# Attention with gates and a multiplicative feed-forward block: quarter products, seven for eight, and blocks of 512 tokens

## The chip, the core and the metric

The kernel runs on one core of a Trainium2 chip. A core has TensorE (matmul, in the profile PE, its weight loads PEld), VectorE (DVE), ScalarE (ACT), GpSimd (POOL) and SyncE (SP, which here issues the DMA transfers). TensorE writes to PSUM, eight banks of 512 f32 columns on 128 partitions; VectorE and ScalarE read PSUM and SBUF. The metric is the device time of one execution in microseconds; lower is better.

## The reference

All in f32, except that the four weight matrices arrive as 8-byte numbers:

```python
f = 1 / (1 + exp(-f_logit))                       # (4, 8, 768, 48)
for t in range(S):
    state = f[t] * state + outer(k[t], v[t])      # one 48 x 48 state for each of 4 x 8 heads
    y[t] = q[t] @ state
x = y, heads side by side                         # 3072 tokens x 384
out = ((x @ w1) * (x @ w2)) @ w3 @ w_out          # 384 -> 1024 -> 1024 -> 384
```

## The kernel before

The sequence is cut into 24 chunks of 128 tokens (`NU`). For a chunk, `attention(u)` makes running products of the gates by two scans on VectorE (L263, L285), scales q and k with them (L279, L293), multiplies K by Q on TensorE (`pa`, L302), copies (L311) and masks the result on GpSimd (L317), multiplies by v and by the state (`py`, L346, L352), and moves the state on (`pk`, L328; `pd`, L368; `S`, L383 and L384). The result goes to `xt` by DMA (or, for the first block, by TensorE through a permutation, L423).

The weights come as 8-byte words and are turned into f32 by ScalarE and VectorE (`fetch`, L566 to L583). w3 and w_out are multiplied once into `wc` (`fold`, L636), so that the feed-forward block has two steps:

- up (L455): for each of 8 groups of 128 hidden features (`jc`) and each of w1 and w2 (`which`), three products, over 384 rows, into one PSUM bank `f`. ScalarE copies the first result (`a`, L464) and VectorE multiplies the second by it (`ab`, L471).
- down (L503): for each 128 tokens, eight products of 384 columns into a bank; ScalarE copies the sum (L516) and SyncE stores it.

Tokens go through it in eight blocks of 384. In the first two blocks the lower half of the hidden features is done chunk by chunk, in products of 128 columns, since a chunk is ready before its block is; all else takes 384 columns. In f32 each product of the code is two instructions on TensorE. PSUM holds `pa` (two banks), `pk`, `pd`, `py` and three banks `f`.

What sets the order is `Plan`: every piece of work is a task with an engine, a cost, tasks that it depends on, a priority and slots that it takes and frees. At each step the task that could start first by the given costs is taken, at equal times the one of lower priority number; the instructions are then written out in that order, so that each engine's queue is fixed at build time and runs in order, with semaphores between the engines.

## Time and profile before

| | us |
|---|---|
| median of 3 runs | 549.43 |
| lowest, highest | 548.67, 550.79 |
| the profiled execution | 546.54 |
| its span, first to last instruction | 544.7 |
| TensorE busy | 522.3 (96%) |
| VectorE busy | 223.1 (41%) |
| ScalarE busy | 164.3 (30%) |

Rows of a group read: line, engine, operation, output from inputs, shapes, count, then busy time in us, mean ns of one, and the engine's idle time before them with what ended it. Rows of the chain or of a timeline begin with start and length in us. Rows of a table of stretches give the stretch, its length, and for PE, PEld, DVE, ACT and POOL the busy us with the number of instructions; then the granted TensorE clock as a share, the DMA share and GB/s.

### The profile page before, as it was taken

To read this page: it belongs to the slowest core of one execution; us is meant where nothing else is said; L and a number is where in the kernel's file an instruction comes from. 1 tells how busy PE (TensorE), PEld (TensorE's weight loads), DVE (VectorE), ACT (ScalarE), POOL (GpSimd) and SP (SyncE) were. 2 spreads that over 40 slices of the span, in tenths; PEclk is the share of its full clock that TensorE was granted. 3 is DMA by queue.
4 is the path that set the end of the run, shared out by engine and by line. 5 is a ranking of instruction groups with operands and counts; after the bars stand their busy time and mean duration, and the time that the engine had idled before them with its cause. 6 is when DMAs were issued, how large, how long until landed. Compare 5 with 4: busy or idle time off the path is not lost.

```text
span 544.7 us, 7379 instructions
## 1 busy us (share of the span) xinstructions
PE 522.3 (96%) x2838; PEld 345.3 (63%) x2838; DVE 223.1 (41%) x351; ACT 164.3 (30%) x325; POOL 40.0 (7%) x45
## 2 busy tenths in 40 slices
PE   2769999999999999999999999999999999999995
PEld 2759866666677965765567556755665555555553
DVE  7699999999767410561326111311011101100100
ACT  3658576542445311441125112311211111111110
POOL 5102010011102000120001000300000000000000
PEclk9999999999999999999999999999999999999998
DMA  6999667754435101330131002100200020000001
GB/s 179 226 238 258 212 228 248 228 159 134 134 113 149 48 0 48 105 110 0 26 91 59 1 10 67 41 1 0 74 16 1 14 58 16 0 14 30 0 16 34
DMA packets 30284, 46.13 MB, mean 85 GB/s; under 512 B 5536, under 2 KB 19744, under 8 KB 29216
## 3 DMA queue, kind: packets, MB, share of 16 engines
q1 hardware_dynamic: 30240, 45.57, 28.8%
q8 instruction: 24, 0.39, 0.3%
q14 instruction: 20, 0.16, 0.1%
HBM read 36.70 MB, written 4.72 MB: 76 GB/s over the span
## 4 chain that ended last, share of the span: by engine, by line
PE 92%; DMA 4%; POOL 1%; SPq 1%; DVE 0%; issue 0%; ACT 0%; POOLq 0%; ACTq 0%
PE f L455 46%; PE f L503 23%; PE f L636 8%; PE pa L302 4%; PE py L346 4%; PE py L352 4%; DMA raw<-in_w_dram 3%; PE pd L368 2%; PE pk L328 2%; DMA q<-in_q_dram 1%; SPq L250 0%; SPq L241 0%; POOL k L196 0%; POOL q L195 0%; PE f L423 0%
## 5 line engine op out<-in xcount | busy, mean ns | idle before, releaser
L455 PE MATMUL f<-xt,w 128*128 128x384 f32 (+1 forms) x960 | 256.3, 427 | 3.0 <-DVE w L583 2.8
L455 PEld LDWEIGHTS f<-xt,w 128*128 128x128 f32 x960 | 161.2, 193 | 89.7 <-DVE w L583 3.0
L503 PE MATMUL f<-wc,ab 128*128 128x384 f32 x384 | 126.2, 486 | 0.0
L471 DVE TENSOR_TENSOR ab<-f,a 128x384 f32<-128x384 f32 (+1 forms) x80 | 37.8, 474 | 204.1 <-PE f L455 203.8
L503 PEld LDWEIGHTS f<-wc,ab 128*128 128x128 f32 x384 | 72.4, 190 | 49.0
L464 ACT COPY a<-f 128x384 f32<-128x384 f32 (+1 forms) x80 | 33.1, 414 | 183.1 <-PE f L455 181.6
L317 POOL TENSOR_SCALAR_AFFINE_SELECT A<-A 128x1024 f32<-128x1024 f32 x24 | 33.1, 1378 | 312.0 <-ACT A L311 312.0
L636 PE MATMUL f<-wos,w3s 128*128 128x384 f32 x128 | 42.9, 488 | 0.0
L516 ACT COPY o<-f 128x384 f32<-128x384 f32 x24 | 11.5, 478 | 85.8 <-PE f L503 85.8
L279 DVE TENSOR_TENSOR Q<-q,fwd 112x512 f32<-112x512 f32 x24 | 18.9, 789 | 41.8 <-PE py L352 41.8
L263 DVE TENSOR_TENSOR_SCAN fwd<-gate,floor 112x512 f32<-112x512 f32 x24 | 31.1, 1294 | 10.1 <-ACT gate L255 8.4
L636 PEld LDWEIGHTS f<-wos,w3s 128*128 128x128 f32 x128 | 23.7, 190 | 14.9
L302 PE MATMUL pa<-Q,K 48*128 48x128 f32 x384 | 29.7, 297 | 1.8 <-DVE K L293 1.8
L285 DVE TENSOR_TENSOR_SCAN bwd<-gate,back 112x512 f32<-112x512 f32 x24 | 31.0, 1293 | 0.8
L302 PEld LDWEIGHTS pa<-Q,K 48*128 48x128 f32 x384 | 25.0, 199 | 7.6 <-issue 4.8
L311 ACT COPY A<-pa 128x1024 f32<-128x1024 f32 x24 | 24.2, 1009 | 16.8 <-PE pa L302 16.6
L346 PE MATMUL py<-A,vt 128*48 128x128 f32 (+1 forms) x384 | 27.2, 284 | 1.3 <-POOL A L317 1.3
L346 PEld LDWEIGHTS py<-A,vt 128*48 128x48 f32 (+1 forms) x384 | 21.3, 133 | 10.9 <-issue 8.7
L396 ACT ACTIVATE ys<-py 112x512 f32<-112x512 f32 x24 | 14.3, 595 | 34.8 <-PE py L352 20.5
L566 ACT ACTIVATE magnitude<-raw 128x1024 f32<-128x1024 f32 (+1 forms) x18 | 19.9, 1108 | 15.6 <-DMA raw<-in_w_dram 9.2
L352 PE MATMUL py<-Q,sb 112*112 112x128 f32 x160 | 22.6, 284 | 0.0
L578 DVE SCALAR_TENSOR_TENSOR rest<-raw 128x1024 uint32<-128x1024 uint32 (+1 forms) x18 | 20.9, 1159 | 0.3 <-DMA q<-in_q_dram 0.2
(55 smaller groups left out, 250.8 us busy)
## 6 DMA issues: line engine op xcount, KB each, us to landing
raw<-in_w_dram SPq DMA_DIRECT2D x8, 1024.0 KB, 5.8
f<-in_f_logit_dram SPq DMA_DIRECT2D x48, 96.0 KB, 2.5
q<-in_q_dram SPq DMA_DIRECT2D x48, 96.0 KB, 2.6
k<-in_k_dram SPq DMA_DIRECT2D x48, 96.0 KB, 2.4
vt<-in_v_dram SPq DMA_DIRECT2D x24, 192.0 KB, 2.6
out_dram<-o SPq DMA_DIRECT2D x24, 192.0 KB, 1.9
raw<-in_w_dram SPq DMA_DIRECT2D x4, 768.0 KB, 9.1
raw<-in_w_out_dram SPq DMA_DIRECT2D x4, 768.0 KB, 5.0
```

What stands on the lines that cost most here:

```text
L263: nc.vector.tensor_tensor_scan(s["P"], gate[u % 2][:, 0:NQ], floor, 0.0, ALU.mult, ALU.max)
L285: nc.vector.tensor_tensor_scan(s["R"][:, ::-1], gate[u % 2][:, NQ:0:-1], back[:, ::-1], 0.0, ALU.mult, ALU.max)
L302: nc.tensor.matmul(s["pa"][:, par, cols], lhsT=s["K"][rows(par), cols], rhs=s["Q"][rows(par), cols], start=True, stop=True,)
L311: nc.scalar.copy(s["A"].rearrange("p r h c -> p r (h c)"), s["pa"])
L317: nc.gpsimd.affine_select(out=a, in_=a, pattern=[[0, H], [1, C]], compare_op=ALU.is_ge, fill=0.0, base=0, channel_multiplier=-1,)
L346: nc.tensor.matmul(s["py"][64 * par : 64 * par + w, hp], lhsT=s["v"][:, h * D : h * D + w], rhs=s["A"][:, par, hp], start=(hp == 0), stop= ...
L352: nc.tensor.matmul(s["py"][:, hp], lhsT=sb[(u - 1) % 2][:, hp], rhs=s["Q"][:, hp * C : hp * C + C], start=False, stop=True, skip_group_che ...
L455: nc.tensor.matmul(s["pu", jc, which, c0][:, 0:nt], lhsT=up_weights(w12, which, kc, jc), rhs=s["xt"][:, kc, cols], start=(kc == 0), stop=( ...
L464: nc.scalar.copy(s["a", jc, c0][:, 0:nt], s["pu", jc, 0, c0][:, 0:nt])
L471: nc.vector.tensor_tensor(s["ab"][jc][:, cols], s["pu", jc, 1, c0][:, 0:nt], s["a", jc, c0][:, 0:nt], ALU.mult)
L503: nc.tensor.matmul(s["po", i], lhsT=s["ab"][jc][:, i * P : i * P + P], rhs=wc[:, jc], start=(jc == 0), stop=(jc == KF - 1),)
L636: nc.tensor.matmul(w3s["p", jc], lhsT=w3s[jc][:, 0, kc * P : kc * P + P], rhs=wos[:, kc], start=(kc == 0), stop=(kc == KF - 1),)
```

## The change

Blocks are 512 tokens, six of them. From block 1 on, the up products of two groups of hidden features (`jc` and `jc + 4`) and of w1 or w2 are made as one unit, `seven(jc, which)`. The 512 tokens are cut into two halves of 256, the two feature groups are the other two halves, and the first two of the three 128-row slices of the input are the halves of the contraction. The four quarter results then come from seven quarter products instead of eight (Winograd's form of Strassen's scheme): m1 to m7, four sums of token quarters (`xs`, L552 of the new code), made once per block, and sums of weight quarters (`w12t`, L953), made once. The third slice of the input takes no part in the scheme and is added by plain products inside m2, m7, m4 and m3, so a unit has 11 products of 256 columns. Three PSUM banks X, Y, Z are used; between products VectorE adds m1 to the banks: u2 after m6 (L605), u3 after m7 (L608), then the results c22, c21, c12 (L619), and c11 by ScalarE or, for w2, as a multiplication (L614). For w2 the results are multiplied by those of w1 (L623). Block 0 uses plain products, and half of block 1 too.

The down step takes 256 tokens at a time, as two halves of 128, the 1024 hidden features as two halves of four groups, and the 384 output columns as two halves of 192: seven times four products of 192 columns, with four sums of hidden quarters for each (`abs_`, L716), sums of `wc` made once (`wct`, L967), and five additions of 192 columns on VectorE (L731 to L765).

`place`, one SBUF tile of 13312 columns, holds the buffers of the weight loading first and those sums later, so the weight sums wait for the last conversion. There are four banks `f` instead of three; `pd` shares the bank of `pk`; k has two buffers instead of three.

Three places of the new order. All rows are those of TensorE (L455, L503 before; L481 after, for all products) or VectorE; an entry in brackets is a wait on another engine's semaphore.

TensorE before, from the last up group to the down step of the last block:

```order
L455 MATMUL f<-xt,w_59 128x384 [waits DVE_49]
L455 MATMUL f<-xt,w_59 128x384 x2
L455 MATMUL f<-xt,w_59 128x384 [waits Activation_49]
L455 MATMUL f<-xt,w_59 128x384 x2
L503 MATMUL f<-wc,ab 128x384 [waits DVE_49]
L503 MATMUL f<-wc,ab 128x384 x6
L503 MATMUL f<-wc,ab 128x384 [waits DVE_49]
```

A wait stands before every third product, for a bank; the last group's eighth down product waits for its own hidden features.

TensorE now, one unit in the middle of block 4 (`w_59` are the weights, `place` the sums). The rows are m2 (two), m7 (two), m1 and m6 of the next unit, m4 (two), m3 (two), and m5 of the next unit:

```order
L481 MATMUL f<-xt,w_59 128x256 [waits Activation_49]
L481 MATMUL f<-xt,w_59 128x256
L481 MATMUL f<-place 128x256
L481 MATMUL f<-xt,w_59 128x256
L481 MATMUL f<-xt,w_59 128x256 [waits DVE_49]
L481 MATMUL f<-place 128x256 [waits DVE_49]
L481 MATMUL f<-xt,place 128x256 [waits DVE_49]
L481 MATMUL f<-xt,place 128x256
L481 MATMUL f<-place,w_59 128x256 [waits DVE_49]
L481 MATMUL f<-xt,w_59 128x256
L481 MATMUL f<-place 128x256 [waits DVE_49]
```

Between m7 and m4, which waits for u3, stand the two first products of the next unit. VectorE at that place, from u3 of a unit of w2 (L608) to u3 of the next:

```order
L608 TENSOR_TENSOR place<-f,a 128x256 [waits PE_49]
L619 TENSOR_TENSOR place<-f,place 128x256 [waits DVE_49]
L623 TENSOR_TENSOR ab<-ab,place 128x256 [waits DVE_49]
L605 TENSOR_TENSOR place<-f,a 128x256 [waits PE_49,Activation_49]
L619 TENSOR_TENSOR a<-f,a 128x256 [waits PE_49]
L623 TENSOR_TENSOR ab<-ab,a 128x256 [waits DVE_49]
L619 TENSOR_TENSOR place<-f,place 128x256 [waits PE_49]
L623 TENSOR_TENSOR ab<-ab,place 128x256 [waits DVE_49]
L608 TENSOR_TENSOR place<-f,a 128x256 [waits PE_49]
```

No work of the attention stands between them here. At the end of block 4, TensorE goes from the last unit (m4, m3) to the down step; its first row is m1 of the down step, which was put ahead of m4:

```order
L481 MATMUL f<-wc,ab 128x192 x3
L481 MATMUL f<-xt,place 128x256 [waits DVE_49]
L481 MATMUL f<-xt,place 128x256
L481 MATMUL f<-place,w_59 128x256 [waits DVE_49]
L481 MATMUL f<-xt,w_59 128x256
L481 MATMUL f<-wc,ab 128x192 [waits Activation_49]
L481 MATMUL f<-wc,ab 128x192 x2
L481 MATMUL f<-wc,ab 128x192 [waits DVE_49]
L481 MATMUL f<-place 128x192 [waits DVE_49]
L481 MATMUL f<-place 128x192 x7
```

VectorE there, c12 of the last unit, its multiplication, and the operand sums of the down step:

```order
L619 TENSOR_TENSOR place<-f,place 128x256 [waits PE_49]
L623 TENSOR_TENSOR ab<-ab,place 128x256 [waits DVE_49]
L716 TENSOR_TENSOR place<-ab 128x512
L716 TENSOR_TENSOR place<-place,ab 128x512 [waits DVE_49]
L716 TENSOR_TENSOR place<-ab,place 128x512 [waits DVE_49]
```

The fourth product of m2 waits for the multiplication, and m6 for the second of the sums; before, the down products waited for one multiplication and no sum.

The diff, cut to its core (`X`, `Y`, `Z` are banks, `wt` a weight quarter, `tw` a sum of weight quarters, `quarter` a token quarter; the down step's m1 to m7 have four products each and the same form):

```diff
-TB = 384
+TB = 512
-NAB = 20
+NF = 4
+DH = DM // 2
+TH = TB // 2
+KH = KF // 2
...
+def place_of(jc):
+    return jc % KH * 2 + jc // KH
...
-    raws = ctx.enter_context(tc.tile_pool(name="raws", bufs=NRAW))
-    abp = ctx.enter_context(tc.tile_pool(name="abp", bufs=NAB))
+    abp = ctx.enter_context(tc.tile_pool(name="abp", bufs=4))
+    outs = ctx.enter_context(tc.tile_pool(name="outs", bufs=4))
-    ps_f = ctx.enter_context(tc.tile_pool(name="ps_f", bufs=3, space=PSUM))
+    ps_f = ctx.enter_context(tc.tile_pool(name="ps_f", bufs=NF, space=PSUM))
...
+    place = keep.tile([P, 13312], F32, name="place")
...
+    raws = [at(2048 * i, 2048).bitcast(U32) for i in range(NRAW)]
+    magnitudes = [at(6144 + 1024 * i, 1024) for i in range(2)]
+    w3_rows = [at(8192 + 1024 * i, 1, 1024) for i in range(2)]
+    wos = at(10240, KF, DM)
+    w12t = place[:, 0:5120].rearrange("p (w t c) -> p w t c", w=2, t=5)
+    xs = at(5120, 4, TH)
+    wct = [at(6144 + KH * DH * i, KH, DH) for i in range(4)]
+    ups = {(nm, i): at(a + 2 * TH * i, TH) for nm, a in (("u2", 9216), ("u3", 9216 + TH)) for i in range(2)}
+    abs_ = [at(10240 + KH * P * i, KH, P) for i in range(4)]
...
-                s["pd"] = ps.tile([R, HP, D], F32, name="pd")
+                s["pd"] = ps.tile([P, HP, R], F32, name="pk")[0:R, :, 0:D]
...
+        def sums():
+            for i in range(4):
+                def emit(i=i):
+                    a11, a12, a21, a22 = quarter(0, 0), quarter(1, 0), quarter(0, 1), quarter(1, 1)
+                    x, y, op = (
+                        (a21, a22, ALU.add), (xs[:, 0], a11, ALU.subtract), (a11, a21, ALU.subtract),
+                        (a12, xs[:, 1], ALU.subtract),
+                    )[i]
+                    nc.vector.tensor_tensor(xs[:, i], x, y, op)
+                deps = [tk[n * UB + c]["x"] for c in range(UB)] if i == 0 else [s["S", i - 1]]
+                last = [q[nm] for q in upq[-KF:] for nm in ("m5", "m6", "m7", "m3")] if i == 0 else []
+                s["S", i] = plan.add("DVE", 0.43, emit, deps + last + w12_sums[-1:], 100 * n + 30)
...
+            def m1():
+                three(bank("X"), [wt(0, 0)], [quarter(0, 0)])
+            def k1():
+                q["a"] = work.tile([P, TB], F32, name="a")[:, 0:TH]
+                nc.scalar.copy(q["a"], q["X"])
+            def m6():
+                three(bank("Y"), [tw(1)], [xs[:, 1]])
+            def m5():
+                three(bank("Z"), [tw(0)], [xs[:, 0]])
+            def m2():
+                three(q["X"], [wt(1, 0), wt(2, 0)], [quarter(1, 0), quarter(2, 0)], False)
+            def m7():
+                three(q["Y"], [tw(2), wt(2, 1)], [xs[:, 2], quarter(2, 1)], False)
+            def m4():
+                three(q["Y"], [tw(3), tw(4)], [quarter(1, 1), quarter(2, 1)], False)
+            def m3():
+                three(q["Z"], [wt(1, 1), wt(2, 1)], [xs[:, 3], quarter(2, 0)], False)
+            def u2():
+                nc.vector.tensor_tensor(ups["u2", k], q["Y"], q["a"], ALU.add)
+            def u3():
+                nc.vector.tensor_tensor(ups["u3", k], q["Y"], q["a"], ALU.add)
+            def c11():
+                if which == 0:
+                    nc.scalar.copy(to(0, 0), q["X"])
+                else:
+                    nc.vector.tensor_tensor(to(0, 0), q["X"], to(0, 0), ALU.mult)
+            def ended(tok, half, bank_, more):
+                def emit():
+                    m = more()
+                    nc.vector.tensor_tensor(m if which else to(tok, half), q[bank_], m, ALU.add)
+                return emit
+            def times(tok, half, more):
+                return lambda: nc.vector.tensor_tensor(to(tok, half), to(tok, half), more(), ALU.mult)
...
+            ready = [tk[n * UB + c]["x"] for c in range(UB)] + pieces[0] + pieces[1]
+            pe("m1", one_, m1, ready + [s["S", 3]] + old(1, "m7"), 0, takes=["f"])
+            q["k1"] = plan.add("ACT", 0.38, k1, [q["m1"]], -200, takes=["a"])
+            pe("m6", one_, m6, [q["m1"]], -1, takes=["f"])
+            pe("m5", one_, m5, [q["m6"]], -1, takes=["f"])
+            dve("u2", u2, [q["k1"], q["m6"]] + old(2, "e12"))
+            pe("m2", two_, m2, [q["k1"], q["m5"]], -5)
+            if which == 0:
+                q["c11"] = takes_ab(jc, plan.add("ACT", 0.38, c11, [q["m2"]], -200, frees=[q["m1"]]))
+            else:
+                dve("c11", c11, [q["m2"]] + old(1, "c11"), frees=[q["m1"]])
+            pe("m7", two_, m7, [q["u2"], q["m2"]], -5)
+            dve("u3", u3, [q["m7"]] + old(2, "e22"))
+            dve("c22", ended(1, 1, "Z", third), [q["u3"], q["m5"], q["c11"]])
+            pe("m4", two_, m4, [q["u3"]], -6)
+            dve("c21", ended(1, 0, "Y", first), [q["m4"], q["c11"]], frees=[q["m6"]])
+            pe("m3", two_, m3, [q["c22"], q["m4"]], -6)
+            dve("c12", ended(0, 1, "Z", second), [q["m3"]], frees=[q["m5"]])
+            if which == 1:
+                for nm, tok, half, more in (("22", 1, 1, third), ("21", 1, 0, first), ("12", 0, 1, second)):
+                    dve("e" + nm, times(tok, half, more), [q["c" + nm]] + old(1, "c" + nm))
+                s["done"][place_of(jc) // KH].extend([q["c11"], q["e22"], q["e21"], q["e12"]])
+            else:
+                for nm in ("22", "21", "12"):
+                    q["e" + nm] = q["c" + nm]
+            q["e21"]["frees"].append(q["k1"])
+            s["up"] += [q[nm] for nm in ("m1", "m2", "m7", "m4", "m3")]
+        if n == 0:
             for c in range(UB):
-                part(c, c + 1, range(KF // 2))
-            part(0, UB, range(KF // 2, KF))
+                part(c, c + 1, range(KH))
+            part(0, UB, range(KH, KF))
         else:
-            part(0, UB, range(KF))
+            if n == 1:
+                for c in range(0, UB, 2):
+                    part(c, c + 2, [jc + half * KH for half in range(2) for jc in range(KH // 2)])
+            for jc in range(KH // 2 if n == 1 else 0, KH):
+                seven(jc, 0)
+                seven(jc, 1)
 
...
+            def sum_(j):
+                def emit():
+                    a11, a21 = quarter_(0, 0), quarter_(1, 0)
+                    if j == 0:
+                        x, y, op = a21, quarter_(1, 1), ALU.add
+                    elif j == 1:
+                        x, y, op = abs_[0], a11, ALU.subtract
+                    elif j == 2:
+                        x, y, op = a11, a21, ALU.subtract
+                    else:
+                        x, y, op = quarter_(0, 1), abs_[1], ALU.subtract
+                    nc.vector.tensor_tensor(abs_[j], x, y, op)
+                return emit
...
+            got0, got1 = (s["done"][i] + wc_sums for i in range(2))
+            got = got0 + got1
+            dve("S0", 0.69, sum_(0), got + old("m5"), -30)
+            dve("S1", 0.69, sum_(1), [q["S0"]] + old("m6", "S3"), -30)
+            dve("S2", 0.69, sum_(2), got0 + old("m7"), -30)
+            dve("S3", 0.69, sum_(3), [q["S1"]] + old("m3"), -30)
+            pe("m1", m1, got0 + old("m7"), takes=["f"])
+            q["k1"] = plan.add("ACT", 0.33, k1, [q["m1"]] + old("c21"), -200)
+            pe("m6", m6, [q["m1"], q["S1"]], -1, takes=["f"])
+            dve("u2", 0.36, u2, [q["k1"], q["m6"]] + old("c12"))
+            pe("m2", m2, [q["k1"]] + got1, -2)
+            q["c11"] = plan.add("ACT", 0.33, c11, [q["m2"]] + stores[-4:-3], -200, frees=[q["m1"]])
+            pe("m7", m7, [q["u2"], q["S2"]], -3)
+            dve("u3", 0.36, u3, [q["m7"]] + old("c22"))
+            pe("m5", m5, [q["S0"], q["m2"], q["m6"]], -3, takes=["f"])
+            dve("c22", 0.36, c22, [q["m5"], q["u3"]] + stores[-4:-2])
+            pe("m4", m4, [q["u3"]], -4)
+            dve("c21", 0.36, c21, [q["m4"], q["c22"]], frees=[q["m6"]])
+            pe("m3", m3, [q["c22"], q["S3"], q["m4"]] + ([judged] if final else []), -4)
+            dve("c12", 0.36, c12, [q["m3"], q["c11"]], frees=[q["m5"]])
+            for half, deps in ((1, ("c21", "c22")), (0, ("c11", "c12"))):
+                stores.append(plan.add("SP", 0.45, store(half), [q[nm] for nm in deps], -10))
...
+        def sum_up(i, which):
+            def emit():
+                t = w12t[:, which]
+                b11, b21, b31, b12, b22, b32 = (
+                    w12[:, half, 2 * which + kc if kc < 2 else 4 + which] for half in range(2) for kc in range(KM)
+                )
+                x, y = ((b12, b11), (b22, t[:, 0]), (b22, b12), (b21, t[:, 1]), (b31, b32))[i]
+                nc.vector.tensor_tensor(t[:, i], x, y, ALU.subtract)
+            return emit
...
+                x, y = ((b12, b11), (b22, wct[0]), (b22, b12), (b21, wct[1]))[i]
```

More of the change, by code (lines that the diff above doesn't have):

```diff
@@ L448, in part @@
             nt = (c1 - c0) * C
-            cost = 6 * max(0.135, nt * 0.322 / TB)
+            cost = 6 * max(0.135, nt * 0.322 / 384)
             def up(jc, which):
@@ L564, in magnitude @@
         def magnitude():
-            s["m"] = flat(work.tile([P, 2 * NW], F32, name="magnitude"))
+            s["m"] = flat(magnitudes[order % 2])
             nc.scalar.activation(s["m"], s["hi"].bitcast(F32), AF.Abs)
```

248 lines of the change are left out of this document (174 added, 74 removed).

## The prediction

> **What bounds the kernel now.** I read the profile's page first (busy shares, chain of waits), then the table of stretches, then the groups of instructions by shape.
>
> ```profile
> span 544.7 us, 7379 instructions
> PE 522.3 (96%) x2838; PEld 345.3 (63%) x2838; DVE 223.1 (41%) x351; ACT 164.3 (30%) x325; POOL 40.0 (7%) x45
> PE 92%; DMA 4%; POOL 1%; SPq 1%; DVE 0%; issue 0%; ACT 0%; POOLq 0%; ACTq 0%
> ```
>
> Nine tenths of the chain that ended last is TensorE. A busy share can hide pipelining, so the stretches (busy us of each engine, granted clock, DMA share) matter more:
>
> ```profile
> 0.00:20.00 20.00, 8.38 (x70) 7.15 (x71) 13.47 (x23) 8.41 (x15) 8.03 (x22) 1.00 0.79 197
> 20.00:40.00 20.00, 14.72 (x144) 13.16 (x143) 16.81 (x26) 12.33 (x22) 1.49 (x1) 1.00 0.92 230
> 40.00:141.00 101.00, 100.98 (x688) 72.15 (x687) 96.61 (x137) 57.83 (x101) 11.56 (x8) 0.98 0.66 205
> 141.00:210.00 69.00, 69.00 (x537) 51.43 (x536) 32.54 (x60) 24.06 (x55) 6.05 (x5) 1.00 0.29 83
> 210.00:479.00 269.00, 269.00 (x1221) 166.29 (x1220) 59.21 (x100) 54.95 (x121) 12.88 (x9) 1.00 0.13 37
> 479.00:539.20 60.20, 60.18 (x187) 35.16 (x185) 4.46 (x8) 6.21 (x13) 0.00 (x0) 1.00 0.05 18
> 539.20:544.70 5.50, 0.00 (x0) 0.00 (x0) 0.00 (x0) 0.48 (x1) 0.00 (x0) 0.74 0.12 42
> ```
>
> From 40 us to 539.2 us TensorE (first busy figure) never stops; all its idle time, some 22 us, lies in the first 40 us and the last 5.5. So every microsecond of products removed after 40 us is a microsecond of the span, and so is every new wait of TensorE. VectorE (third figure) is nearly full from 40 to 141 us too, yet TensorE did not wait there. Afterwards it has room.
>
> **The price of a product by its columns.** Each product in the code is two instructions in the trace (480 up products, x960). The chain shows runs of them back to back; a group taken from 53 to 61.5 us gives the narrow ones:
>
> ```profile
> 448.23 30.96 PE f L455 x96
> 479.19 15.48 PE f L503 x48
> 48.50 1.34 PE f L423 x12
> L455 PE MATMUL f<-xt,w 128*128 128x128 f32 x75 | 8.5, 275 | 0.0
> L455 PEld LDWEIGHTS f<-xt,w 128*128 128x128 f32 x76 | 8.6, 192 | 0.1
> ```
>
> 384 columns: 30.96 / 96 = 322.5 ns per instruction. 128 columns: 8.5 / 75 = 113 ns. (The means, 275 here, contain the latency and overlap; busy time over count is the spacing.) Widths 192 and 256 do not occur. Bounds: in proportion to the columns, 161.3 and 215.0; on the straight line through the two rows, 165.4 and 217.8. I take the middle, 163.5 and 216.5; 512 columns in proportion, 430.
>
> The weight load, 192 ns in its row, might be thought to bind at 163.5. It does not: loads of that length followed each other every 113 ns in that very row, so they overlap. The Trainium skill, page "TensorE: Matmul & The Clock Gate", section "Back-to-back issue gap", speaks against this change: in a stream of loads and matmuls the spacing is set by both, 81 ns at 128 columns and 131 at 512. By that flat curve an instruction of 192 columns would cost an estimated 78% of one of 384, not half, and the change would lose. The row disagrees, 113 against 322.5 being 35%, so the sum goes by the row.
>
> **Products removed and added** (counts from the order of instructions, two instructions each):
> - before: 336 up products of 384 columns, 216.7 us; 144 of 128, 32.5; 192 down products of 384, 123.8. Together 373.0.
> - after: 96 of 128, 21.7; 24 of 512, 20.6; 444 of 256, 192.3; 336 down products of 192, 109.9. Together 344.5, so 28.5 less.
>
> The gain is below an eighth for three reasons: block 0 and half of block 1 still use plain products; the third slice of the 384 input rows takes no part, so a unit is 11 products instead of 12; only the down part gets 28 for 32. One chunk more goes through the moving products of L423, 1.34 us: net **27.2 us** less (24.9 to 30.1 by the bounds).
>
> **What is added on VectorE.** Rows by shape:
>
> ```profile
> L471 DVE TENSOR_TENSOR ab<-f,a 128x384 f32<-128x384 f32 x56 | 31.1, 556 | 193.1 <-PE f L455 192.7 <-ACT a L464 0.4
> L471 DVE TENSOR_TENSOR ab<-f,a 128x128 f32<-128x128 f32 x24 | 6.7, 283 | 11.1 <-PE f L455 11.1
> L383 DVE TENSOR_TENSOR S<-pd,S 112x192 f32<-112x192 f32 x16 | 5.6, 353 | 9.3 <-PE pd L368 9.3
> L263 DVE TENSOR_TENSOR_SCAN fwd<-gate,floor 112x512 f32<-112x512 f32 x24 | 31.1, 1294 | 10.1 <-ACT gate L255 8.4 <-ACT lasts L268 1.0
> L285 DVE TENSOR_TENSOR_SCAN bwd<-gate,back 112x512 f32<-112x512 f32 x24 | 31.0, 1293 | 0.8
> L293 DVE TENSOR_TENSOR K<-k,bwd 112x512 f32<-112x512 f32 x24 | 18.0, 750 | 4.9 <-DMA k<-in_k_dram 2.5 <-PE pa L302 1.8
> L279 DVE TENSOR_TENSOR Q<-q,fwd 112x512 f32<-112x512 f32 x24 | 18.9, 789 | 41.8 <-PE py L352 41.8
> ```
>
> 256 columns lie halfway between 283 and 556: 0.42 us. 192 columns: 0.353. 512: 0.75. The 36 units need 252 operations of 256 (five in a unit of w1, nine in one of w2): 106 us. Twelve down groups of four sums and five additions: 12 x (3.0 + 1.77) = 57. The remaining plain products 10.8, sums of tokens 20 x 0.42 = 8.4, sums of weights 10 x 0.75 and 4 x 1.1 = 12. Together 194, less the 37.8 of the two first rows: VectorE grows from 223 to about 379 us, some 71% of the new span. It stays below TensorE on average; what counts is where it comes last.
>
> **Inside a unit.** In the steady part one unit is 22 instructions, 22 x 216.5 = 4.76 us, with 5.9 us of VectorE per two units (9.5 us). The tightest wait is m4 for u3, a sum from PSUM that can start only when m7 is done. How long a hand-over takes:
>
> ```profile
> 447.75 0.49 PE L503 MATMUL f<-wc,ab 128*128 128x384 f32 x1
> 448.07 8.23 PE L455 MATMUL f<-xt,w 128*128 128x384 f32 x25
> 448.27 0.48 ACT L516 COPY o<-f 128x384 f32<-128x384 f32 x1 [4.68 <-PE f L503]
> ...
> 38.39 0.52 ACT kt L336
> 38.95 0.67 PE pd L368 x14
> ```
>
> The reader starts 0.20 us after the next product could start (448.27 against 448.07), and TensorE starts 0.04 after an engine that it waits for (38.91 to 38.95). So m4 is free 0.20 + 0.42 + 0.04 = 0.66 us after m7. The new order puts m1 and m6 of the next unit there, 4 x 0.2165 = 0.87 us: covered. By the same count c22 is ready for m3 (1.1 us against 1.7), and c21 frees its bank for the next m5 at 2.44 against 2.60. That last margin, 0.16, is shorter than a weight load of 192 ns, which may be sent late: I take 0.05 per unit, 1.8 us for 36 (0 to 3.6). Were a unit's next one not there to cover, it would cost 0.66 each, 24 us.
>
> **At a block's end.** The last unit has no successor ready. After its m3 come c12 and its product with the other factor, then two sums of 512, before the down product m6 has its operand: 0.20 + 0.42 + 0.42 + 0.75 + 0.75 + 0.04 = 2.58 us, against m2's four products, 8 x 0.1635 = 1.31. TensorE idles 1.27 us, and everything queued behind m6 waits with it. Four blocks: **5.1 us**; block 1 has plain products there, up to 1.3 more.
>
> **After the last fold.** Up to it the order is nearly the same on both engines, so I leave the first 141 us alone. From there to the first unit, TensorE has ten chunks of attention, the second half of block 0, its down part and the plain half of block 1. A chunk from the chain:
>
> ```profile
> 141.73 1.02 PE py L346 x15
> 142.75 1.06 PE py L352 x8
> 143.81 0.59 PE pd L368 x14
> 144.40 1.09 PE pa L302 x16
> 145.50 0.54 PE pk L328 x4
> ```
>
> In the new order that is about 34 us of attention, 12 x 0.86 = 10.3, 56 x 0.327 = 18.3 and 24 x 0.433 = 10.4: 73 us. VectorE has ten chunks of about 5.2 us (scans, K, Q, state) and 17 us of sums: 69 us. Two engines 5% apart, tied by waits both ways. Lower bound of the loss 0, since the stretch 40:141 above held 96.61 and 100.98 of 101; upper bound 13, if VectorE gets through 80% (69 / 0.8 - 73). The nearest row is that stretch: I take **3**. The later bursts of four chunks between blocks (VectorE 31 us, TensorE 38) get **2** (0 to 5).
>
> **The sum.** 544.7 - 27.2 + 1.8 + 5.1 + 3 + 2 = 529.4 us of span; 1.8 lie around it (546.54 - 544.7), so 531.2 for a profiled execution. The runs' median stands 2.9 above the profiled one (549.43 against 546.54): **534 us**. The tail of 5.5 us stays: a copy of 0.48 gives way to an addition of 0.35 after the last product.
>
> **The rivals.**
> - *Nearly all of it arrives.* The order fills the gaps, new waits come to 3 us: 534 - 9 = 525. For it: no wait of TensorE in 499 us before. Against: the block's end is a chain that no other work covers. Chance 0.17.
> - *VectorE is late, slower than before.* It runs in order; a scan of 1.29 us that stands ahead of u3, c22 or an operand sum holds TensorE. Place: the 20 units of blocks 1 to 3 and the 8 down groups of blocks 0 to 3, while attention lasts. At one scan each, 28 x 1.29 = 36 us: 549.4 - 27.2 + 6.9 + 36 = 565. From 20.3 / 28 = 0.73 us per piece it turns the change into a loss; half of it is a draw, 547. For it: 69 against 73 us after the folds. Against: between units the new VectorE order holds almost no attention. Chance 0.13, half of that near the draw.
> - *The weight load binds narrow products.* At 190 ns instead of 163.5 for 672 down instructions: 17.8 us, 552. The 113 ns row speaks against it. (It is the flat curve of the Trainium skill, same page and section, as far as rows of this kernel can price it.) Chance 0.04.
> - *The forecast*, new waits between 5 and 22 us, 527 to 544: chance 0.62. The remaining 0.04 is a stall at the start (one buffer less for k, a shared bank for pk and pd).
>
> **How the numbers follow.** The range reaches down to all of the saving with little waiting, 523, and up to 547, where a late VectorE eats it. A change within 0.5%, 546.7 to 552.2, is about what cannot be told from none. Faster: forecast, first rival and a little of the second, 0.80. Same: 0.09. Slower: 0.11.
>
> **What would show it.** Right: spacing near 163 and 216 ns for 192 and 256 columns; about 4.8 us per unit in the last two blocks; gaps of TensorE of 1 to 1.5 us before the first down m6 of a block, put down to DVE; VectorE near 380 us. Wrong: 190 ns or more in the down runs; gaps before m4 in every unit; TensorE idle over 10 us between 141 and 220 us with VectorE full; a first unit later than some 220 us.

## The result, and the profile after

The changed kernel takes 529.1 us (median of 4 runs, 528.4 to 530.4) where the kernel before takes 549.1 beside it: ratio 0.963, 95% interval 0.960 to 0.966, 20.0 us less. The forecast was 534 us, range 523 to 547. A later repeat gave 527.9 against 549.3, ratio 0.961 (0.958 to 0.963).

The page of the profiled execution (530.42 us): span, busy time of each engine, and the shares of the chain that ended last.

```profile
span 528.7 us, 8629 instructions
PE 497.6 (94%) x3306; PEld 423.3 (80%) x3306; DVE 369.4 (70%) x693; ACT 157.6 (30%) x328; POOL 40.0 (8%) x44
PE 77%; DMA 10%; DVE 5%; SPq 4%; POOL 1%; ACT 1%; issue 1%; DVEq 0%; POOLq 0%; ACTq 0%
```

TensorE has lost 24.7 us of busy time and VectorE has gained 146. TensorE still leads the chain, but it is no longer free of waits. The stretches of the changed kernel show where:

```profile
40.00:141.00 101.00, 97.46 (x693) 70.21 (x692) 95.36 (x138) 58.88 (x99) 10.08 (x7) 0.98 0.65 200
141.00:180.00 39.00, 38.77 (x312) 28.84 (x312) 35.49 (x58) 14.40 (x33) 6.66 (x4) 1.00 0.32 88
180.00:220.00 40.00, 40.00 (x385) 35.40 (x384) 31.20 (x54) 20.39 (x46) 6.00 (x5) 1.00 0.50 148
...
260.00:340.00 80.00, 78.56 (x572) 69.28 (x568) 52.60 (x109) 20.72 (x51) 6.29 (x5) 1.00 0.17 49
340.00:430.00 90.00, 88.27 (x460) 79.86 (x460) 49.47 (x122) 9.44 (x27) 0.00 (x0) 1.00 0.08 24
```

Idle (stretch less the first figure behind it): 3.5 us from 40 to 141 (0.0 before); only 0.2 from 141 to 220, where VectorE is busy for 35.5 of 39 and then for 31.2 of 40 us; and 1.4 and 1.7 in the two stretches that hold block ends. The table of waits of TensorE names the latter (total us, times, longest):

```profile
PE f L481 <- DVE place L716: 2.9, 4, 0.7
PE py L382 <- DMA vt<-in_v_dram: 0.8, 1, 0.8
PE py L986 <- DVE good L984: 0.6, 1, 0.6
PE f L481 <- DVE place L744: 0.5, 1, 0.5
```

**The spacing of products.** The timeline of TensorE, m2 of a unit and of the third unit behind it:

```profile
408.61 1.03 PE L481 MATMUL f<-xt,w 128*128 128x256 f32 x4
...
422.85 1.03 PE L481 MATMUL f<-xt,w 128*128 128x256 f32 x4
```

(422.85 - 408.61) / 3 = 4.747 us for 22 instructions, 215.8 ns each with no gap between the units. The down part has eight instructions of 192 columns in each row here, and one such row between the two:

```profile
454.37 1.46 PE L481 MATMUL f<-place,ab 128*128 128x192 f32 x8
...
456.97 1.46 PE L481 MATMUL f<-wc,ab 128*128 128x192 f32 x8
```

2.60 / 16 = 162.5 ns. Weight loads of 190 ns (the mean of their rows) bind neither. The Trainium skill, page "TensorE: Matmul & The Clock Gate", section "Wait — 56ns, not 53.3ns?", has one matmul start N / 2.4 GHz + about 2.5 ns after the last. If each of the two f32 instructions streams its columns twice, which no run here shows apart, that makes an estimated 162.5 and 215.8 ns for 192 and 256 columns; the trace agrees with both. With the flat curve of the same page that the prediction weighed, it does not.

**A block's end.** Around the last unit of block 4 in the changed kernel (m2 of the down part from 446.60, m6 from 449.07; L619 is c12, L623 its product with the other factor, L716 the operand sums):

```profile
446.60 1.73 PE L481 MATMUL f<-wc,ab 128*128 128x192 f32 x8
446.80 0.42 DVE L619 TENSOR_TENSOR place<-f,place 128x256 f32<-128x256 f32 x1
447.26 0.43 DVE L623 TENSOR_TENSOR ab<-ab,place 128x256 f32<-128x256 f32 x1
447.60 0.69 DVE L716 TENSOR_TENSOR place<-ab 128x512 f32<-128x512 f32 x1
448.32 0.69 DVE L716 TENSOR_TENSOR place<-place,ab 128x512 f32<-128x512 f32 x1
449.07 4.17 PE L481 MATMUL f<-place 128*128 128x192 f32 x24 [0.73 <-DVE place L716]
...
453.07 1.46 PE L481 MATMUL f<-wc,ab 128*128 128x192 f32 x8
```

From 446.60 to 453.07 lie 32 instructions, 5.20 us at 162.5 ns, in 6.47: 1.27 us are lost. The wait in brackets, 0.73, is smaller, since the rows count the tail of the pipeline as busy. (The 1.33 us in some expectations below were counted from m2's last weight load instead.)

### The profile page after: what moved, and what is told of

Same layout as the page of the kernel before. It is cut to its first block, busy times and chain, and to the rows that moved or that the text cites. A ratio compares the mean times of both kernels' runs of the same rounds, so it can differ in the third digit from the quotient of the medians.

```text
span 528.7 us, 8629 instructions
## 1 busy us (share of the span) xinstructions
PE 497.6 (94%) x3306; PEld 423.3 (80%) x3306; DVE 369.4 (70%) x693; ACT 157.6 (30%) x328; POOL 40.0 (8%) x44
## 4 chain that ended last, share of the span: by engine, by line
PE 77%; DMA 10%; DVE 5%; SPq 4%; POOL 1%; ACT 1%; issue 1%; DVEq 0%; POOLq 0%; ACTq 0%
PE f L481 57%; PE f L921 8%; DMA place<-in_w_dram 5%; PE pa L338 4%; PE py L382 3%; PE py L388 3%; DMA f<-in_f_logit_dram 2%; SPq L451 2%; PE pk L404 2%; PE pk L364 1%; DVE place L716 1%; DMA vt<-in_v_dram 1%; SPq L448 1%; DMA place<-in_w_out_dram 1%; DVE ab L623 0%
## 5 line engine op out<-in xcount | busy, mean ns | idle before, releaser
L481 PE MATMUL f<-xt,w 128*128 128x256 f32 (+2 forms) x696 | 163.6, 369 | 3.6 <-DVE w L868 3.6
L481 PEld LDWEIGHTS f<-xt,w 128*128 128x128 f32 x696 | 118.7, 194 | 25.3 <-issue 9.6
L481 PE MATMUL f<-place 128*128 128x192 f32 (+1 forms) x504 | 114.1, 350 | 2.9 <-DVE place L716 2.9
L481 PEld LDWEIGHTS f<-place 128*128 128x128 f32 x504 | 87.7, 190 | 9.8 <-DVE place L716 4.1
L921 PE MATMUL f<-place 128*128 128x384 f32 x128 | 43.0, 489 | 0.0
L481 PE MATMUL f<-xt,place 128*128 128x256 f32 x144 | 37.1, 380 | 0.0
L481 PE MATMUL f<-wc,ab 128*128 128x192 f32 x192 | 36.5, 330 | 0.0
L921 PEld LDWEIGHTS f<-place 128*128 128x128 f32 x128 | 23.7, 190 | 15.7 <-issue 0.6
L608 DVE TENSOR_TENSOR place<-f,a 128x256 f32<-128x256 f32 x36 | 15.3, 425 | 28.9 <-PE f L481 28.9
L481 PEld LDWEIGHTS f<-wc,ab 128*128 128x128 f32 x192 | 31.7, 190 | 1.9 <-DVE ab L623 1.2
L481 PEld LDWEIGHTS f<-xt,place 128*128 128x128 f32 x144 | 27.0, 189 | 3.7
L382 PEld LDWEIGHTS py<-A,vt 128*64 128x64 f32 (+1 forms) x384 | 21.8, 135 | 8.1 <-issue 5.2
L850 ACT ACTIVATE place<-place 128x1024 f32<-128x1024 f32 (+1 forms) x18 | 20.0, 1113 | 17.8 <-DMA place<-in_w_dram 9.3
```

What stands on the lines that cost most here:

```text
L382: nc.tensor.matmul(s["py"][64 * par : 64 * par + w, hp], lhsT=s["v"][:, h * D : h * D + w], rhs=s["A"][:, par, hp], start=(hp == 0), stop= ...
L481: nc.tensor.matmul(out_, lhsT=lhs[i], rhs=rhs[i], start=start and i == 0, stop=i == len(lhs) - 1, skip_group_check=True,)
L608: nc.vector.tensor_tensor(ups["u3", k], q["Y"], q["a"], ALU.add)
L850: nc.scalar.activation(s["m"], s["hi"].bitcast(F32), AF.Abs)
L921: nc.tensor.matmul(w3s["p", jc], lhsT=w3s[jc][:, 0, kc * P : kc * P + P], rhs=wos[:, kc], start=(kc == 0), stop=(kc == KF - 1),)
```

## The experiments

Times are medians; each is compared with the kernel before on its own chip, and "us from 529.1" is then to be read with about 1.6 us of uncertainty. A sharper measure came out of the traces. From the start of the last fold (the last group of 16 products of 384 columns before 141 us) to the end of the last product, two executions of the kernel before, and two of the changed one, agree to 0.1 us (two rows each, in that order):

```profile
136.39 5.34 PE L636 MATMUL f<-wos,w3s 128*128 128x384 f32 x16
523.53 15.64 PE L503 MATMUL f<-wc,ab 128*128 128x384 f32 x48
```
```profile
138.50 5.34 PE L636 MATMUL f<-wos,w3s 128*128 128x384 f32 x16
529.83 11.45 PE L503 MATMUL f<-wc,ab 128*128 128x384 f32 x35
```
```profile
138.08 5.43 PE L921 MATMUL f<-place 128*128 128x384 f32 x16
521.65 1.46 PE L481 MATMUL f<-wc,place 128*128 128x192 f32 x8
```
```profile
135.06 5.43 PE L921 MATMUL f<-place 128*128 128x384 f32 x16
518.52 1.46 PE L481 MATMUL f<-wc,place 128*128 128x192 f32 x8
```

Before: 402.78 and 402.78 us. Changed: 385.03 and 384.92. Below it is called "from the fold to the end", 385.0 for the changed kernel. Between the two kernels it is not an exact measure, since the change also moves work across the fold; among kernels that have the same work ahead of the fold it is.

### Is the cover between m7 and m4 what pays?

m1 and m6 of the next unit are held back until m4 is out (the order of VectorE, ScalarE and SyncE stays the same):

```diff
+    late = {}
+    for a, b in zip(upq, upq[1:]):
+        late[id(b["m1"])] = late[id(b["m6"])] = a["m4"]
...
+        # a task of late, and what depends on it, is written out behind that m4
     for t in plan.order():
         t["emit"]()
```

> Same instructions as the changed kernel on every engine; only TensorE's order differs: in each pair of neighbouring units of a block (31 pairs) m1 and m6 of the next unit now come behind m4 instead of between m7 and m4. Theory (the seven products are paid for by the cover between m7 and m4): TensorE waits 0.66 us (0.20 + 0.42 + 0.04) before each m4, 31 x 0.66 = 20.5 us more than the changed kernel's 529.1: about 549.5 us (547 to 553), and the wait stands in the trace before m4, put down to VectorE. Rival (the number of TensorE's instructions sets the time, and the order in a unit does not matter, since instructions are queued ahead): under 5 us more, 529 to 534.

Measured: 560.8 us, ratio 1.019 (1.014 to 1.024); without the cover the change is a loss. The sign and the place are the theory's; the size lies above its range (547 to 553) and is half as much again as forecast, 31.7 us or 1.02 per pair of units instead of 0.66. The timeline of TensorE in this kernel, one unit (m7 from 429.66, m4 at 431.20, m5 of the next unit at 434.12):

```profile
430.09 0.59 PE L481 MATMUL f<-xt,w 128*128 128x256 f32 x2
431.20 1.13 PE L481 MATMUL f<-xt,place 128*128 128x256 f32 x4 [0.52 <-DVE place L608]
432.17 0.59 PE L481 MATMUL f<-xt,w 128*128 128x256 f32 x2
...
433.47 0.59 PE L481 MATMUL f<-xt,w 128*128 128x256 f32 x2
434.12 0.70 PE L481 MATMUL f<-place 128*128 128x256 f32 x2
434.65 1.03 PE L481 MATMUL f<-xt,w 128*128 128x256 f32 x4
```

m7's last instruction could be followed at 430.09 + 0.43 = 430.52; m4 starts 0.68 us later: the 0.66 of the prediction. Then come three costs that it did not have. m4's four instructions take 0.97 us to the next one instead of 0.86, so the first instruction behind a wait costs 0.11 more. m5 starts 0.22 late (434.12 against 433.90), since c21, which frees its bank, stands behind the next unit's u2 in VectorE's queue, and u2 now waits for the late m1 and m6. And m5 itself then takes 0.10 more. Together 1.11 for this pair of units. The rival, that TensorE's count of instructions alone decides, falls.

### Does VectorE's total count, or the place of its work?

Each of 36 units gets one VectorE instruction more, the same sum with the same operands, once beside the tight chain and once in it:

```diff
 def u2():
-    nc.vector.tensor_tensor(ups["u2", k], q["Y"], q["a"], ALU.add)
+    for _ in range(2):
+        nc.vector.tensor_tensor(ups["u2", k], q["Y"], q["a"], ALU.add)
```

> The sum u2 of each of the 36 units runs twice on VectorE (the second time with the same result): 36 x 0.46 = 16.6 us more of VectorE's work. Theory (what counts on VectorE is only the chain m7, u3, m4, which u2 is not on; m7, which needs u2, stands some 3 us behind it): 0 to 3 us more, 529 to 532. Rival (VectorE's total binds the units, since its queue is full or in order): up to 16.6 more, 540 to 546.

Measured: 532.0 us, ratio 0.970 (0.967 to 0.973), 2.9 more than the changed kernel; from the fold to the end 2.7 more. So 36 more sums of 0.46 us each (VectorE's busy time rises by 11.9 us) cost less than 3 us. Where they cost is m5's wait for c21 (the prediction's margin of 0.16 us), behind which u2 now stands longer:

```profile
416.25 0.88 DVE L606 TENSOR_TENSOR place<-f,a 128x256 f32<-128x256 f32 x2
416.95 0.59 PE L481 MATMUL f<-xt,w 128*128 128x256 f32 x2
417.05 0.41 DVE L620 TENSOR_TENSOR a<-f,a 128x256 f32<-128x256 f32 x1
417.52 0.70 PE L481 MATMUL f<-place 128*128 128x256 f32 x2
```

m5 could start at 416.95 + 0.43 = 417.38 and starts at 417.52. Now the same in u3:

```diff
 def u3():
-    nc.vector.tensor_tensor(ups["u3", k], q["Y"], q["a"], ALU.add)
+    for _ in range(2):
+        nc.vector.tensor_tensor(ups["u3", k], q["Y"], q["a"], ALU.add)
```

> The sum u3 of each of the 36 units runs twice instead, the same 16.6 us of VectorE as u2 twice. Theory: m4 is then ready 0.66 + 0.46 = 1.12 us after m7, and m1 and m6 of the next unit cover 0.87: 0.25 us of wait in each of 31 pairs, 7.8 us more: 537 us (534 to 540), with the wait before m4. Rival (VectorE's total binds): the same as u2 twice. Rival (large slack in the units): under 531.

Measured: 539.7 us, ratio 0.984 (0.981 to 0.987), 10.6 more than the changed kernel; from the fold to the end 11.2 more. The same instruction costs four times as much here. Rows of that kernel (L609 is u3, twice; 425.23 and 430.36 are m4 of two units in a row):

```profile
424.29 0.88 DVE L609 TENSOR_TENSOR place<-f,a 128x256 f32<-128x256 f32 x2 [1.27 <-PE f L481]
424.52 0.59 PE L481 MATMUL f<-place 128*128 128x256 f32 x2
425.23 1.13 PE L481 MATMUL f<-xt,place 128*128 128x256 f32 x4
...
430.36 0.92 PE L481 MATMUL f<-xt,place 128*128 128x256 f32 x3
```

A unit now takes 5.13 us instead of 4.75. m6 of the next unit, from 424.52, covers to 424.95; m4 starts 0.28 later (0.25 expected), and 0.10 are the dearer first instruction behind a wait. 0.38 x 31 = 11.8, close to the 11.2. The rival that VectorE's total binds would have given both runs the same time and falls.

### What do the two parts, and the blocks of 512, bring apart?

Up by seven, down plain (down products of 384 columns, as before the change):

```diff
-        for i in range(UB // 2):
-            q = down(i)
+        for i in range(UB):
+            plain_down(i)      # cut here: 8 products of 384 columns, then one copy and one store
...
-            pe("m1", one_, m1, ready + [s["S", 3]] + old(1, "m7"), 0, takes=["f"])
+            pe("m1", one_, m1, ready + downq[-1:] + [s["S", 3]] + old(1, "m7"), 0, takes=["f"])
```

> Only the up part by seven products; the down part is plain (192 products of 384 columns instead of 336 of 192), without the four sums per group. Theory: products cost 123.8 - 109.9 = 13.9 us more, and the four waits of 1.33 us at the block ends go, since the plain down part needs no operand sums: 529.1 + 13.9 - 5.3 = 537.7 us (535.5 to 540). Rival (the block ends' waits come from the last unit itself and not from the operand sums): 543 us.

Measured: 538.7 us, ratio 0.979 (0.975 to 0.984, which is 535.5 to 540.4 us). Close to the theory's 537.7; the rival's 543 lies outside. Its trace has no wait for operand sums, but one that the expectation lacks: with plain down products behind it the last unit of a block has no cover for its own m4. In so far the rival has a part in it.

```profile
PE f L481 <- DVE place L608: 2.1, 4, 0.5
```

(The sums of `wc`, which nothing uses here, are left out as well.)

Down by seven, up plain (and without the sums of the weights of w1 and w2):

```diff
-            for jc in range(KH // 2 if n == 1 else 0, KH):
-                seven(jc, 0)
-                seven(jc, 1)
+            part(0, UB, [jc + half * KH for jc in range(KH // 2 if n == 1 else 0, KH) for half in range(2)])
```

> Only the down part by seven; the up part is plain in blocks of 512 tokens. Theory: 36 units of 22 instructions at 215.7 ns (170.8 us) become 72 plain up groups of 6 instructions at 430 (185.8): 15.0 us more. The block's end shrinks: from the last up product 0.20 + 0.75 + 0.72 + 0.72 + 0.04 = 2.43 us to m6's operand, against m1 and m2 of the down part, 2.6 us, if both lie behind that product: 0 to 1.1 us of wait instead of 1.33 in each of four. 529.1 + 15.0 - (0.9 to 5.3) = 538.8 to 543.2, middle 541. Rival (VectorE's sums in the units hold the changed kernel back elsewhere, which plain up products would set free): under 537.

Measured: 535.7, 537.6 and 538.8 us, ratio 0.976 (0.970 to 0.982) from these three executions. A fourth took 1353.6 us. The kernel has a second path for inputs that its range test (`judge`) rejects; whether that execution took it is not on record, so its cause stays open. The three lie at or just below the lower edge of what was expected (538.8), and the interval (532.6 to 539.7 us) reaches below 537 too, so the times alone do not separate theory and rival. The trace does more: no wait for an operand sum at a block's end, and from the fold to the end 393.4. To compare this with the changed kernel, one piece of work has to be added: K by Q of one chunk stands ahead of the last fold here, and behind it in the changed kernel (224 of its instructions begin behind the fold's start here, 240 there):

```profile
135.34 1.16 PE L338 MATMUL pa<-Q,K 48*128 48x128 f32 x16
136.43 5.43 PE L922 MATMUL f<-place 128*128 128x384 f32 x16
```

With its 1.09 us the stretch is 394.5, 9.5 more than in the changed kernel, against 9.7 expected for a block's end that is fully covered.

Neither, only blocks of 512 with all the new buffers: both edits above together.

> Blocks of 512 tokens with all the changed buffers, but plain products in both parts. Theory: 529.1 + 15.0 + 13.9 - 5.3 = 552.7 us, about 3.6 above the kernel before (549.1), because the 3.3 us that TensorE idles more in the first 141 us come from the new buffers and not from the products; its trace then idles about 20 us up to 141 us. Rival (those 3.3 us are chance between two executions, or belong to the seven products): 549 us, with about 17 us idle up to 141.

Measured: 550.8 us, ratio 1.002 (0.999 to 1.004). It lies between the two expectations and its interval holds the rival's 549 (1.000) and not the theory's 552.7 (1.006). Up to 141 us its TensorE idles 17.2 us, as little as the kernel before in its first profile. So blocks of 512 alone change the time by at most 0.4%, and nothing here shows that the new buffers make the start longer.

From the fold to the end the four read 407.0 (neither: 405.9 and the same 1.09 for K by Q, which stands ahead of the fold there too), 395.4 (up), 394.5 (down) and 385.0 (both). Up alone brings 11.6, down alone 12.5, both 22.0: 2.1 less than the sum. It fits that the block ends' waits for operand sums appear only where units are followed by quarter products; that they are the whole of the 2.1 was not tested apart.

### Can a block's end be covered?

m1 of the second down group needs only the first half of the hidden features and is ready long before. In blocks 2 to 5 it goes between m2 and m6 of the first group:

```diff
             q = down(i)
+            if i == 1 and n >= 2:
+                q["m1"]["deps"] = [d for d in q["m1"]["deps"] if d is not downq[-2]["m7"]] + [downq[-2]["m2"]]
+                downq[-2]["m6"]["deps"].append(q["m1"])
```

(and the next block's first product waits for this group's m5, so that the four banks f cannot lock).

> The changed kernel, and in blocks 2 to 5 m1 of the second down group moves from behind the first group to between its m2 and m6 (nothing added or removed). Theory (TensorE idles 1.33 us at these four block ends because it has nothing while the last unit's sums and the two operand sums run): m1, 1.30 us, fills that gap, 4 x 1.3 = 5.2 us less: 529.1 - 5.2 = 524 us (522.5 to 525.5), and the waits of m6 for the operand sums fall below 0.1 us each. Rival (the wait moves: the second group lacks m1 as cover later, or banks come free later): 528 to 530 us, with new waits inside the down groups.

Measured: 527.3 us, ratio 0.961 (0.958 to 0.964), 1.8 less than 529.1 and the same ratio as the changed kernel's repeat: no gain that the medians can tell. The traces can: from the fold to the end it takes 381.6, 3.4 less than the changed kernel, where 5.2 were expected. The rival was half right. At the block's end of this kernel:

```profile
445.31 3.03 PE L481 MATMUL f<-wc,ab 128*128 128x192 f32 x16
448.17 4.06 PE L481 MATMUL f<-place 128*128 128x192 f32 x24
...
452.54 1.54 PE L481 MATMUL f<-place 128*128 128x192 f32 x8 [0.30 <-DVE place L717]
```

The loss before the first m6 shrinks from 1.27 to 0.26 us (448.17 - 445.31 - 16 x 0.1625), but m6 of the second group now comes 0.47 late (452.54 - 448.17 - 24 x 0.1625): its S0 may not be written before m5 of the first group has read the same buffer. With a second buffer for S0, and m1 of the second group already before m2 of the first:

```diff
+    second_sum = keep.tile([P, KH, P], F32, name="second_sum")
...
+            first_sum = second_sum if i and n >= 2 else abs_[0]
...
-            dve("S0", 0.69, sum_(0), got + old("m5"), -30)
+            dve("S0", 0.69, sum_(0), got + ([downq[-3]["m5"]] if n >= 3 or n == 2 and i else old("m5")), -30)
...
+            if i == 1 and n >= 2:
+                q["m1"]["deps"] = [d for d in q["m1"]["deps"] if d is not downq[-2]["m7"]] + [downq[-2]["m1"]]
+                downq[-2]["m2"]["deps"].append(q["m1"])
```

> The earlier move alone, m1 of the second down group as cover in blocks 2 to 5, took 1.8 us off the median instead of 5.2: its trace shows m6 of the second group waiting 0.30 us for its operand sum, because S0 of the second group had to wait for m5 of the first, which reads the same buffer. Here S0 of the second group has a buffer of its own (three instead of four for the rows of the output make room), and m1 of the second group stands before m2 of the first. No product or sum is added. Theory (each block end's wait was kept alive by that buffer): all four waits of 1.33 us go, 529.1 - 5.3 = 523.8 us (522.5 to 525.5), and neither m6 waits more than 0.1 us. Rival (the block's end is bound by the chain of sums on VectorE as a whole, whose wait turns up at the next product): 526 to 528, with a wait before m4 or m7 of these groups.

Beside it ran the changed kernel, with no edit:

> The changed kernel once more, beside the one with two sums, so that a difference of 1 per cent is seen on the same chip. Expected: 529 us (527.5 to 530.5). Its start: if the idle time of TensorE up to 141 us is chance between executions, it may lie anywhere from 17 to 21 us here; if it belongs to the kernel, 20 again.

Measured: 521.8 us against 527.9 for the changed kernel on the same chip; ratios to the kernel before 0.951 (0.948 to 0.953) and 0.961 (0.958 to 0.963). That is 6.1 us less, and this kernel beats both. From the fold to the end it saves 5.2 (379.7 against 384.9), four block ends of 1.3, as the theory has it; the median lies just below the expected 522.5 to 525.5, which fits the start, where executions scatter (in the two traces the last fold begins at 133.87 and 135.06). The same place in its trace (L713 writes S0, for the second group into the new buffer; L721 the other operand sums):

```profile
440.35 2.76 PE L482 MATMUL f<-wc,ab 128*128 128x192 f32 x16
442.07 0.69 DVE L721 TENSOR_TENSOR place<-place,ab 128x512 f32<-128x512 f32 x1
442.95 5.36 PE L482 MATMUL f<-place 128*128 128x192 f32 x32
443.41 0.68 DVE L713 TENSOR_TENSOR second_sum<-ab 128x512 f32<-128x512 f32 x1
448.15 1.46 PE L482 MATMUL f<-place,ab 128*128 128x192 f32 x8
```

440.35 to 448.15 is 7.80 us for 48 instructions: 162.5 ns each, nothing lost. The sums end at 442.76, 0.2 us before m6 needs them. No work was taken away; the products only stand in another order.

### Does the start belong to the change?

In its profile the changed kernel idled 3.3 us more than the kernel before up to 141 us (20.2 against 16.9). Two runs look for the reason. Three buffers for k again:

```diff
-    outs = ctx.enter_context(tc.tile_pool(name="outs", bufs=4))
+    outs = ctx.enter_context(tc.tile_pool(name="outs", bufs=3))
...
-        t["lk"] = plan.add("SP", 0.85, load(ks[u % 2], k), past(u, 2, "k"), n0 - 28, lag=2.0)
+        t["lk"] = plan.add("SP", 0.85, load(ks[u % 3], k), past(u, 3, "k"), n0 - 28, lag=2.0)
```

> The changed kernel with three buffers for k again as before the change (and three instead of four for the rows of the output, for the room). Theory (the 3.3 us more of TensorE's idle time in the first 141 us come from weight transfers that took longer to issue, 6.03 us against 4.22 for the eight at 30 us, and not from the k buffer): 528.5 to 530.5, idle time up to 141 us still about 20 us. Rival (a load of k that waits for the product before it holds the queue): 526 us, idle about 17 us.

Measured: 529.6 us, ratio 0.965 (0.963 to 0.968); idle up to 141 us 19.8. No gain: it is not the buffer. (That the issue of the weight transfers makes the difference, as the theory says, this run does not show.) And the kernel before once more, with no edit:

> The kernel before once more, for a second profile of its start. Theory (the 3.3 us at the start are chance between executions, as the start's idle time of 17.2 to 21.1 us in the kernels that share the changed kernel's first 141 us suggests): idle time up to 141 us between 16 and 20 us, not 16.9 again to the tenth. Rival (the start of the kernel before is steadily shorter): 16.5 to 17.3.

Measured: 548.2 us, ratio 0.999 (0.996 to 1.001). The stretch up to 141 us in the first profile of the kernel before, in the second, and in the two of the changed kernel:

```profile
0.00:141.00 141.00, 124.08 (x897) 92.46 (x898) 126.89 (x184) 78.57 (x136) 21.08 (x31) 0.99 0.72 207
```
```profile
0.00:141.00 141.00, 120.81 (x890) 90.36 (x891) 124.82 (x181) 77.98 (x135) 20.92 (x31) 0.99 0.74 207
```
```profile
0.00:141.00 141.00, 120.79 (x889) 91.38 (x890) 124.45 (x183) 77.16 (x131) 19.56 (x29) 0.98 0.71 200
```
```profile
0.00:141.00 141.00, 122.90 (x898) 91.89 (x899) 126.89 (x186) 77.97 (x133) 18.74 (x29) 0.99 0.69 200
```

Idle 16.9 and 20.2 before (just above the 16 to 20 expected), 20.2 and 18.1 after; the other nine kernels lie from 17.2 to 21.1. The kernel before alone spans the 3.3 us, so they need no other cause than scatter between executions, and nothing here shows them to be a price of the change. Idle time need not agree with the time lost, since the same work ahead of the fold is counted as busy up to 1.2 us longer in one execution than in the other: the last fold begins at 136.39 and 138.50 in the kernel before, at 138.08 and 135.06 in the changed one.

## Why the prediction was right

- **Sign, place and mechanism** held: TensorE's chain sets the end, so removed products come off the span, and VectorE's 146 us more (156 were forecast) stay under TensorE's work. The run without the cover shows on what that hangs: with m4 right behind m7 the gain becomes a loss.
- **The price by columns** (163.5 and 216.5 ns taken between the bounds): 162.5 and 215.8. With these the products come to 343.1 us instead of 344.5, and the net saving to 28.6 instead of 27.2.
- **Late weight loads**, 1.8 us: nothing in the units looked at. From the m2 of one to that of the third behind it there is no gap. The tight place was named rightly, c21 before m5; it costs only once VectorE's queue is longer there.
- **Block ends**, 1.27 each: 1.27 in the trace, and 5.2 for the four when they were covered. That the hundredths agree is chance: the operand sums take 0.69 us each instead of 0.75, so m6 starts 0.1 sooner, and its first instructions then take 0.1 more (24 take 4.00 us instead of 3.90).
- **After the last fold**, 3 us taken of 0 to 13: 0.2 of idle time. From the fold's end to the first unit (143.34 to 216.4) the stretch took 73 us, as counted; the 34 us of attention in it are less than ten whole chunks, since some pieces of the first and last chunks lie outside. VectorE ran there at 35.5 of 39 and then 31.2 of 40 us without holding TensorE. **Later bursts**, 2 us: waits for v by DMA 0.8, for the range test 0.6, for u3 of the last down group 0.5. The sum is as forecast, but by luck: only the first stands in a burst, and it is a late load of v; no burst held TensorE because VectorE was behind.
- **The first 141 us**, taken as unchanged: right on average, but the two profiles that were compared differ by 3.3 us of scatter.
- **The sum**: -28.6 + 5.1 + 0.2 + 2 = -21.3 by these readings, against -20.0 and -21.4 in the two comparisons of medians and -15.3 forecast. So the gain was underrated by 5 to 6 us: 2.8 in the stretch behind the fold, 1.8 in weight loads, 1.4 in the prices. That the span came out as forecast, 528.7 against 529.4, is partly luck. The two profiled spans differ by 16.0 us: from the fold to the end 17.8 were saved (402.8 against 385.0), and the changed kernel's fold began 1.7 later. In the second pair of profiles it began 3.4 earlier (135.06 against 138.50), and the spans differ by 20.6. By the counts of instructions TensorE has about 2 us less to do ahead of the fold, so that the readings put some 19.3 of the 21.3 behind it, an estimate; of these, 1.5 did not arrive, and no row was found for them.
- **The 2.9 us** added for the runs' median over the profiled execution made most of the distance from 534 to 529.1: the median of the changed kernel stands 1.3 below its profiled execution, not 2.9 above. The profiled execution of the kernel before was the quickest of its runs, that of the changed kernel (530.42) the slowest. An offset of one pair of numbers does not carry over when its cause is scatter, here, as far as the profiles show, that of the start.
- **The rivals.** "Nearly all of it arrives" (525) was a little nearer than the forecast (4.1 us against 4.9), but not for its reason: the block ends did stay uncovered. "VectorE is late" priced a late piece at a scan each; no unit showed one. What was mis-sized there, and in the 24 us for a missing cover, is the price of a wait: 1.0 to 1.1 us for one that was put at 0.66, since the products behind it start dearer and one more sum is pushed back. "The weight load binds" is refuted by 162.5 ns.

## What to carry to other kernels

In this kernel the products saved on the full engine paid only where the sums that they need instead were covered by products that do not wait for them. So count, for each sum read back from PSUM, the hand-over, its length and the products that stand between. Total busy time of the helping engine says little (36 equal sums cost 2.9 us in one place and 10.6 in another). At the seams, where a stage ends and the cover with it, look for a product that is ready early, and check that the buffer of its operands is free early too; here that brought 6 us without removing any work.

## What the hardware showed that was not expected

- A wait of TensorE costs more than its length: the first instruction of 256 columns behind it takes some 0.32 us to the next instead of 0.216 (0.97 for four instead of 0.86; likewise 0.53 for two instead of 0.43). Its weight load of 0.19 us has nothing to hide behind; that this is the cause was not tested apart. One row speaks for it: in the changed kernel eight instructions of 192 columns right behind products of 48 columns, where the profile names no wait, take 1.41 us (158.34 to 159.75) instead of 1.30, and there too the first load starts only with its product.
- The start, where weights and inputs are loaded, scatters between two executions of one kernel: the last fold began 2.1 us apart in the kernel before and 3.0 in the changed one, while the 385 and 403 us behind the last fold's start repeat to 0.1 us in both. Comparisons below 1% are better made from a mark in the trace behind the start.
